# Reordering the first steps, regrouping the last batch and moving the last residuals in a top-k attention and MLP kernel

## The chip, the cores and the metric

The program runs on one core of a Trainium2 chip. The metric is the device time of one execution in microseconds; lower is better. The engines are named as the profile names them: PE is TensorE (PEld is its loading of weights), DVE is VectorE, ACT is ScalarE, POOL is GpSimd and SP is SyncE, which issues most of the DMAs.

## The reference, cut to what matters

There are 8 batches, 8 heads, 576 rows and a head size of 64, all in float32. For each row the 32 largest of 576 scores are kept, and the rest take no part in the softmax. The heads are laid side by side (512 columns), and a normalised MLP of width 2048 with a residual follows. `moe_g_ln` and the two weight matrices arrive as float64.

```python
scores = scale * np.matmul(q, k.transpose(0, 1, 3, 2))
kth = np.partition(scores, -top_k, axis=-1)[..., -top_k:-top_k + 1]
scores = np.where(scores >= kth, scores, -1000000000.0)
attn = np.exp(scores - np.max(scores, axis=-1, keepdims=True))
attn = attn / (np.sum(attn, axis=-1, keepdims=True) + 1e-09)
x = np.matmul(attn, v)                       # then heads side by side: (8, 576, 512)
xn = (x - mu) / np.sqrt(var + 1e-06) * g_ln
out = x + np.maximum(xn @ w_ch1, 0.0) @ w_ch2
```

## The kernel before, in words

**Tiles, jobs and units.** The 576 rows of a batch are four tiles of 128 rows, numbered 0 to 3, and a rest of 64 rows, numbered `J` (4). Two heads are handled together, so a batch has four head pairs (`hp`). A *unit* is one row tile of one head pair; a *group* is the list of tiles whose attention is multiplied with the values at once; a *job* is one group of one head pair. `parts` says how a batch is cut: batch 0 in `[0,1]`, `[2,3]`, `[J]`; batch 1 in `[0,1]`, `[2,3,J]`; batches 2 to 7 in `[0,1,J]`, `[2,3]`. For each part all four head pairs come in turn, which gives N = 160 units.

**The steps.** The program is one long loop over steps `n`, written out by hand; each engine executes its own instructions in the order in which they are issued. In step `n`, unit `n` goes through `select` on DVE, in four calls; unit `n+1` is prepared for it; earlier units are masked, exponentiated, turned and multiplied with the values. The parts that matter here are:

- `scores(u)`: eight products on PE into four PSUM tiles (L354), which ACT copies to `sc` (L335). `due(n)` says whose scores step `n` makes: those of unit n+1 in the early steps, of unit n+2 after step 17.
- `halve(u)`: of the two halves of every row of scores, DVE takes the elementwise maximum `hi` (L375); POOL works out the minimum `lo` from integers, as a subtraction and an addition (L376, L379).
- `select(u, 0)` takes 16 candidates out of `lo`; `select(u, 1)` to `select(u, 3)` take the 32 largest out of `hi` and those candidates (MAX8 and MATCH_REPLACE8, L391, L386, L399).
- `move(u)` turns a unit's weights by two DVE transposes (L468) and DMAs through DRAM, `turn(u)` by PE transposes (L490) and ACT copies (L502). A unit is `moved` from batch 2 on, if it is neither a rest nor the last of its group.
- `values(g)` multiplies a group with its values (L544, L551); `place(g)` turns the result back and puts it into `x` (L583, L560).

**The weights.** Each of 32 pieces of the float64 weights is converted by the kernel: `fetch` (a DMA), `split` (three or four ACT operations L183 to L189, then a clamp on POOL, L190), `shift` (a left shift by three bits on DVE, L193) and `join` (two POOL operations, L199 and L201). `batches` puts four pieces ahead of the loop and then one or two into each of the steps 0 to 15; `weights(n, 0)` and `weights(n, 1)` issue them. The shifts and joins of a batch are issued one step after its splits, in `weights(n, 1)`, after `halve(nxt)`.

**The MLP and its planner.** When all four head pairs of a part are done, their rows become a `Block` of one to three row tiles. `give(n)` puts its products into the list `todo`: transposes of `x` ("turn"), 64 products for the hidden layer ("hidden", L664) whose moving side has 128 columns for each tile of the block, and 16 products of 512 columns for each tile ("project", L680). After the last product of a tile, ACT scales (L689), POOL adds the residual (L693), and SP stores. Eight calls of `fill()` in every step take products out of `todo`: each call adds `share[0]` to a credit `owed[0]`, which is held at 6.0 at most, and products are issued while the credit covers half their planned cost. `slot(n)` sets the share. Up to step 17 it is the difference of planned DVE and PE costs; after that it spreads what is in `todo` evenly over the steps up to each coming give, keeps a reserve of 4 us, and takes the least of these:

```python
                if m > n:
                    even = min(even, (left - RESERVE) / (m - n))
                    left += sum(b.cost() for b in gives[m])
```

The first block is given at step 9 (`gives_first`), the others at 19, 31, 44, 55 and so on; the last two of batch 7 are a block of three tiles (tiles 0 and 1 with the last rows of batches 6 and 7) at step 156 and a block of two at step 163. The loop ends with step 165.

**The lead-in.** Before the loop the kernel loads, turns and scores the first head pair, calls `halve(units[0])`, `load_gain()` and the splits of the four first pieces (`weights(-1, 0)`, `weights(-1, 1)`).

Of the kernel before, what the change touches and what calls it, by code (L numbers as in the profile page):

```python
# [10 lines left out]
ALU = mybir.AluOpType  # L11
# [10 lines left out]
J = 4  # L22
# [7 lines left out]
def kernel(  # L30
# [41 lines left out]
    nc = tc.nc  # L72
    P = nc.NUM_PARTITIONS
    B, H, S, D = q.shape
# [130 lines left out]
    now = [-1]  # L205
# [5 lines left out]
    def load_gain():  # L211
        ps = turned()
        nc.tensor.transpose(ps[:, 0:NC], grow[:], ident[0:NC, 0:NC])
        nc.scalar.copy(gcol[:], ps[:, 0:NC])


    batches = {}
# [5 lines left out]

    def weights(n, phase):

        now, before = batches.get(n, []), batches.get(n - 1, [])
        if phase == 0:
            for x in batches.get(n + 1, []):
                x.fetch()
            for x in now[0::2]:  # L230
                x.split()
        elif phase == 1:
            for x in before:
                x.shift()
            for x in before:
                x.join()
            for x in now[1::2]:
                x.split()
# [5 lines left out]
    share = [0.0]  # L244
    owed = [0.0]
# [83 lines left out]
    def scores(u):  # L329

        u.sc = scpool.tile([P, 2, S], FP32, tag="sc", name="sc")
        made = [score_half(u, s) for s in range(2)]
        for t in range(len(u.tiles)):
            for s in range(2):
                nc.scalar.copy(  # L335
                    u.sc[:, t, s * HALF : (s + 1) * HALF], made[s][t][:, 0:HALF]
                )
# [25 lines left out]
    def halve(u):  # L363

        nt = len(u.tiles)  # L370
        u.lo = lopool.tile([P, 2, HALF], FP32, tag="lo", name="lo")
        u.hi = hipool.tile([P, 2, HALF + TOP_K // 2], FP32, tag="hi", name="hi")
        a, b = u.sc[:, 0:nt, 0:HALF], u.sc[:, 0:nt, HALF:S]
        lo, hi = u.lo[:, 0:nt], u.hi[:, 0:nt, 0:HALF]
        nc.vector.tensor_tensor(hi, a, b, ALU.max)  # L375
        nc.gpsimd.tensor_tensor(  # L376
            lo.bitcast(I32), a.bitcast(I32), hi.bitcast(I32), ALU.subtract
        )
        nc.gpsimd.tensor_tensor(lo.bitcast(I32), lo.bitcast(I32), b.bitcast(I32), ALU.add)  # L379
# [215 lines left out]
    class Block:  # L595
# [40 lines left out]
        def items(self):  # L636
            n = self.n
            N = n * P
# [38 lines left out]
            def project(i, f):  # L677
                if f == 0:
                    ps[i] = product("ops")
                nc.tensor.matmul(  # L680
                    ps[i][:],
                    hT[f][:, i * P : (i + 1) * P],
                    w2[:, f, :],
                    start=(f == 0),
                    stop=(f == NF - 1),
                )
                if f == NF - 1:
                    o = opool.tile([P, DM], FP32, tag="o", name="o")
                    nc.scalar.activation(  # L689
                        o[:], ps[i][:], AF.Identity,  # L690
                        bias=self.mv[:, i, 0:1], scale=self.rstd[:, i : i + 1],
                    )
                    nc.gpsimd.tensor_tensor(o[:], o[:], self.x[i], ALU.add)  # L693
                    for dst, rows in self.dsts[i]:
                        stores.append(lambda d=dst, s=o[rows, :]: nc.sync.dma_start(d, s))

# [33 lines left out]
    for b in range(B):  # L730
        parts = [[0, 1], [2, 3], [J]]
        if b:
            parts = [[0, 1], [2, 3]]
            parts[b < 2].append(J)
        for qts in parts:
            jobs += [Job(b, hp, [qts]) for hp in range(NHP)]
    units = []
# [7 lines left out]
    N = len(units)  # L745
# [11 lines left out]
    CONVERTING = max(n for n in batches if batches[n]) + 2  # L757
# [16 lines left out]
    for j in jobs:  # L774
        if j.hp == NHP - 1:
            b = j.b
# [23 lines left out]
    def at(i):  # L800
        return units[i] if 0 <= i < N else None
# [6 lines left out]

    def due(n):

        ahead = [n + 1] if n < CONVERTING else [n + 2]
        if n == CONVERTING:
            ahead = [n + 1, n + 2]
        return [units[i] for i in ahead if i < N]
# [5 lines left out]
    for j in fresh[1:]:  # L820
        before = jobs[jobs.index(j) - 1]
# [32 lines left out]
    def slot(n):  # L854


        if n <= CONVERTING:
            return max(0.0, dve_cost(n) - pe_cost(n)) / SLOTS
        left = sum(t[1] for t in todo)
        if n > last_give:  # L860
            even = left / max(1, END - 1 - n)
        else:
            even = 99.0
            for m in sorted(gives):
# [3 lines that stand above are left out]
        return max(0.0, even) / SLOTS  # L868
# [8 lines left out]
    gives_first = min(gives)  # L877
# [7 lines left out]
    load(fresh[1], nc.sync, nc.scalar)  # L885
    scores(units[0])
    halve(units[0])
    load_gain()
    weights(-1, 0)
    weights(-1, 1)  # L890
    for n in range(END):
        now[0] = n
        if n in gives:
            give(n)
        share[0] = slot(n)
        u, nxt, mk = at(n), at(n + 1), at(n - 1)
        ex, g = after(n)
        g = g if g and not g.quick else None
# [38 lines left out]
            keep_den(ex)  # L937
        if u:
            select(u, 1)
        if nxt:  # L940
            halve(nxt)
        for den in recips.pop(n, []):
# [101 lines left out]
```

## Time and profile before

| What | Before |
| --- | --- |
| Device time, median of 4 runs | 1660.4 us (1657.11 to 1660.88) |
| Device time of the profiled execution | 1660.76 us |
| Span of the profiled execution | 1658.3 us |
| Granted PE clock, mean | 0.978 |
| PE busy | 1560.5 us, 94% of the span |
| DVE busy | 1474.5 us, 89% |
| ACT busy | 1038.0 us, 63% |
| POOL busy | 675.0 us, 41% |

The span is measured from the first to the last instruction in the profile; the device time is 2.5 us more in the same execution. Times below are in microseconds from the start of the span unless a duration is meant. A row of the timeline gives the start, the length, the engine, the line, the operation with its output and inputs, the number of instructions, and in brackets how long the engine stood idle before it and who ended that. PE matmul rows overlap: each instruction's end is modelled, so the spacing from one start to the next tells the rate.

### The profile page before, as it was taken

To read this page: it belongs to the slowest core of one execution; us is meant where nothing else is said; L and a number is where in the kernel's file an instruction comes from. 1 tells how busy PE (TensorE), PEld (TensorE's weight loads), DVE (VectorE), ACT (ScalarE), POOL (GpSimd) and SP (SyncE) were. 2 spreads that over 40 slices of the span, in tenths; PEclk is the share of its full clock that TensorE was granted. 3 is DMA by queue.
4 is the path that set the end of the run, shared out by engine and by line. 5 is a ranking of instruction groups with operands and counts; after the bars stand their busy time and mean duration, and the time that the engine had idled before them with its cause. 6 is when DMAs were issued, how large, how long until landed. Compare 5 with 4: busy or idle time off the path is not lost.

```text
span 1658.3 us, 24475 instructions
## 1 busy us (share of the span) xinstructions
PE 1560.5 (94%) x6825; PEld 919.2 (55%) x6825; DVE 1474.5 (89%) x4619; ACT 1038.0 (63%) x2607; POOL 675.0 (41%) x879
## 2 busy tenths in 40 slices
PE   2668989989899999999999999999999999999998
PEld 1336457456455475755547575655547565755564
DVE  5997999999999999999999999999999999997000
ACT  6886877767656666666656665666656665665310
POOL 5776763343333434334343433344343433343010
PEclk9879999999999999999999999999999999999999
DMA  7423333001433334333443325333443334232100
GB/s 177 105 71 95 88 60 62 22 14 23 95 104 97 92 87 120 100 101 79 120 114 102 86 80 138 91 92 84 115 118 98 86 83 122 90 92 72 32 13 13
DMA packets 301199, 142.28 MB, mean 86 GB/s; under 512 B 246276, under 2 KB 283144, under 8 KB 301064
## 3 DMA queue, kind: packets, MB, share of 16 engines
q1 hardware_dynamic: 296328, 140.13, 31.9%
q10 hardware_dynamic: 4736, 0.59, 0.3%
q8 instruction: 55, 0.90, 0.2%
q14 instruction: 80, 0.66, 0.1%
HBM read 93.46 MB, written 47.19 MB: 85 GB/s over the span
## 4 chain that ended last, share of the span: by engine, by line
PE 66%; DVE 20%; ACT 5%; issue 4%; POOL 2%; DMA 1%; SPq 0%; ACTq 0%; POOLq 0%; DVEq 0%
PE hps L664 24%; PE ops L680 23%; PE scps L354 8%; PE av L544 6%; DVE m L399 6%; DVE hi L386 5%; DVE hi L391 3%; PE av L551 2%; PE tp L490 2%; DVE lo L386 2%; DVE hi L375 2%; ACT e L426 1%; ACT sc L335 1%; DVE size L193 1%; PE tp L648 1%
## 5 line engine op out<-in xcount | busy, mean ns | idle before, releaser
L664 PE MATMUL hps<-xT,w 128*128 128x256 f32 (+1 forms) x2048 | 551.4, 413 | 6.2 <-ACT xT L653 6.2
L680 PE MATMUL ops<-w,h 128*128 128x512 f32 x1152 | 548.8, 603 | 0.0
L399 DVE MAX8 m<-hi 128x8 f32<-128x304 f32 x1152 | 489.1, 461 | 3.3
L664 PEld LDWEIGHTS hps<-xT,w 128*128 128x128 f32 x2048 | 373.2, 192 | 122.7 <-issue 31.9
L376 POOL TENSOR_TENSOR lo<-sc,hi 128x576 int32<-128x576 int32 (+1 forms) x160 | 208.2, 1301 | 481.9 <-DVE hi L375 238.2
L386 DVE MATCH_REPLACE8 hi<-m,hi 128x304 f32<-128x304 f32 x864 | 390.6, 458 | 0.0
L680 PEld LDWEIGHTS ops<-w,h 128*128 128x128 f32 x1152 | 200.7, 192 | 186.4 <-issue 181.4
L354 PE MATMUL scps<-kT,qT 64*128 64x288 f32 (+3 forms) x1344 | 219.8, 429 | 35.3 <-DVE qT L306 26.5
L391 DVE MAX8 hi<-lo 128x8 f32<-128x288 f32 x576 | 234.0, 443 | 12.8 <-POOL lo L379 11.7
L335 ACT COPY sc<-scps 128x288 f32<-128x288 f32 x576 | 199.7, 408 | 70.9 <-PE scps L354 56.5
L426 ACT ACTIVATE e<-sc,m 128x576 f32<-128x576 f32 x288 | 224.1, 779 | 6.1 <-DVE m L399 4.0
L436 ACT ACTIVATE e<-e,bias 128x576 f32<-128x576 f32 x288 | 224.8, 781 | 0.6
L379 POOL TENSOR_TENSOR lo<-lo,sc 128x576 int32<-128x576 int32 (+1 forms) x160 | 207.3, 1296 | 12.6
L354 PEld LDWEIGHTS scps<-kT,qT 64*128 64x128 f32 (+1 forms) x1344 | 122.0, 179 | 152.3 <-issue 60.3
L675 ACT ACTIVATE h<-hps 128x512 f32<-128x512 f32 (+1 forms) x160 | 89.2, 557 | 95.3 <-PE hps L664 94.1
L544 PE MATMUL av<-pt,vb 128*64 128x256 f32 (+2 forms) x1088 | 147.8, 414 | 0.2 <-ACT pt L513 0.2
L375 DVE TENSOR_TENSOR hi<-sc 128x576 f32<-128x576 f32 (+1 forms) x160 | 116.7, 729 | 21.9 <-ACT sc L335 21.9
L386 DVE MATCH_REPLACE8 lo<-hi,lo 128x288 f32<-128x288 f32 x288 | 125.6, 443 | 0.0
L693 POOL TENSOR_TENSOR o<-o,x 128x512 f32<-128x512 f32 x32 | 42.2, 1320 | 199.9 <-ACT o L689 199.9
L556 ACT COPY oT<-av 128x256 f32<-128x256 f32 (+2 forms) x68 | 26.2, 386 | 148.9 <-PE av L551 148.9
L544 PEld LDWEIGHTS av<-pt,vb 128*64 128x64 f32 x1088 | 73.8, 142 | 77.9 <-ACT sc L335 15.9
L490 PE MATMUL tp<-ident,e 128*128 128x128 f32 x576 | 92.1, 285 | 25.0 <-ACT e L436 24.5
(70 smaller groups left out, 1257.9 us busy)
## 6 DMA issues: line engine op xcount, KB each, us to landing
turned<-sc SPq DMA_DIRECT2D x72, 512.0 KB, 2.6
pt<-turned SPq DMA_DIRECT2D x288, 128.0 KB, 3.0
vb<-in_v_dram SPq DMA_DIRECT2D x136, 128.0 KB, 2.7
raw<-in_moe_w_ch_dram SPq DMA_DIRECT2D x32, 512.0 KB, 4.0
kin<-in_k_dram SPq DMA_DIRECT2D x128, 72.0 KB, 2.6
qin<-in_q_dram SPq DMA_DIRECT2D x120, 72.0 KB, 2.7
out_dram<-o SPq DMA_DIRECT2D x32, 256.0 KB, 2.2
ends<-in_v_dram SPq DMA_DIRECT2D x136, 16.0 KB, 2.4
```

Of the source, the lines that this page charges most:

```text
L335: nc.scalar.copy(u.sc[:, t, s * HALF : (s + 1) * HALF], made[s][t][:, 0:HALF])
L354: nc.tensor.matmul(ps[i * R : i * R + ql, o : o + width], qT[r, q0 : q0 + ql], kT[r, k0 : k0 + width], start=True, stop=True,)
L376: nc.gpsimd.tensor_tensor(lo.bitcast(I32), a.bitcast(I32), hi.bitcast(I32), ALU.subtract)
L379: nc.gpsimd.tensor_tensor(lo.bitcast(I32), lo.bitcast(I32), b.bitcast(I32), ALU.add)
L386: nc.vector.match_replace(x[:, t], m[:, t, :], x[:, t], LOWEST)
L391: nc.vector.max(u.hi[:, t, o : o + 8], u.lo[:, t])
L399: nc.vector.max(m[:, t, :], u.hi[:, t])
L426: nc.scalar.activation(u.e[:, t], u.sc[:, t], AF.Prelu, bias=u.thr[:, t, 7:8], scale=-1.0, alpha=SLOPE)
L436: nc.scalar.activation(u.e[:, t], u.e[:, t], AF.Exp, bias=u.bias[:, t : t + 1], scale=-scale / SLOPE, accum_out=g.den[:, col : col + 1],)
L544: nc.tensor.matmul(av[h * D : (h + 1) * D, 0 : g.nq], vb[:, h * J + c, :], g.blocks[:, h, 0 : g.nq // 32, c, :], start=(c == 0), stop=False,)
L664: nc.tensor.matmul(ps["h"][:, o : o + N], w1[:, c, f * P : (f + 1) * P], xT[0][:, c, 0:N], start=(c == 0), stop=(c == NC - 1),)
L680: nc.tensor.matmul(ps[i][:], hT[f][:, i * P : (i + 1) * P], w2[:, f, :], start=(f == 0), stop=(f == NF - 1),)
```

## The change

It has five parts.

1. The scores of unit 1 are issued ahead of the loop, right after `halve(units[0])` and before `load_gain()` and the splits of the first four pieces; `due(0)` is empty.
2. For unit 0 alone, `lo` is made by DVE as a minimum instead of by two POOL operations.
3. The shifts of a batch of pieces leave `weights(n, 1)` and are issued in step `n` after `select(u, 1)` and before `halve(nxt)`.
4. In step `gives_first` (9) the credit `owed[0]` is set to zero and the share is halved.
5. The last batch is cut in `[0,J]`, `[1,2]`, `[3]` instead of `[0,1,J]`, `[2,3]`: twelve jobs instead of eight, still twenty units. Its blocks have two tiles (tile 0 and the last rows), two tiles (1 and 2) and one tile (3), given at steps 152, 159 and 163. Residuals issued after step N (160) are added by DVE instead of POOL.

```diff
@@ weights
         elif phase == 1:
-            for x in before:
-                x.shift()
             for x in before:
                 x.join()
@@ halve
         nc.vector.tensor_tensor(hi, a, b, ALU.max)
+        if u.i == 0:
+            nc.vector.tensor_tensor(lo, a, b, ALU.min)
+            return
         nc.gpsimd.tensor_tensor(
             lo.bitcast(I32), a.bitcast(I32), hi.bitcast(I32), ALU.subtract
         )
@@ project
-                    nc.gpsimd.tensor_tensor(o[:], o[:], self.x[i], ALU.add)
+                    engine = nc.vector if now[0] > N else nc.gpsimd
+                    engine.tensor_tensor(o[:], o[:], self.x[i], ALU.add)
@@ jobs
         if b:
             parts = [[0, 1], [2, 3]]
-            parts[b < 2].append(J)
+            if b == B - 1:
+                parts = [[0, J], [1, 2], [3]]
+            else:
+                parts[b < 2].append(J)
@@ due
-        ahead = [n + 1] if n < CONVERTING else [n + 2]
+        ahead = [] if n == 0 else [n + 1] if n < CONVERTING else [n + 2]
@@ lead-in
     scores(units[0])
     halve(units[0])
+    scores(units[1])
     load_gain()
@@ loop
         share[0] = slot(n)
+        if n == gives_first:
+            owed[0] = 0.0
+            share[0] /= 2
...
         if u:
             select(u, 1)
+        for x in batches.get(n - 1, []):
+            x.shift()
         if nxt:
             halve(nxt)
```

## The prediction

> **What bounds the kernel now.** I read the page's 40 slices first, to see where an engine is short of work.
>
> ```profile
> PE   2668989989899999999999999999999999999998
> ...
> DVE  5997999999999999999999999999999999997000
> ...
> PEclk9879999999999999999999999999999999999999
> ```
>
> Three stretches differ. In the first tenth PE has gaps while DVE is full; then both are full; in the last 120 us PE works alone. The sums by stage put numbers to it (columns: window, length, then PE, PEld, DVE, ACT and POOL busy with instruction counts, granted clock, DMA share, GB/s).
>
> ```profile
> 10.00:20.00 10.00, 2.76 (x11) 1.37 (x9) 4.78 (x15) 8.17 (x17) 4.64 (x5) 1.00 0.88 203
> 20.00:30.00 10.00, 2.29 (x8) 1.26 (x8) 5.91 (x7) 7.32 (x15) 5.75 (x6) 1.00 0.49 113
> ...
> 130.00:140.00 10.00, 10.00 (x44) 8.67 (x43) 5.86 (x23) 4.23 (x8) 4.51 (x5) 0.93 0.17 52
> 480.00:1500.00 1020.00, 1015.03 (x4470) 591.09 (x4467) 1005.35 (x3159) 649.64 (x1676) 397.23 (x557) 1.00 0.36 99
> 1530.00:1653.00 123.00, 123.00 (x413) 70.79 (x411) 3.93 (x10) 27.05 (x59) 8.10 (x12) 1.00 0.06 19
> ```
>
> From 480 us PE lacks 5 us in 1020, and from 1530 on it lacks none. The end is therefore PE's: the time is PE's work plus PE's gaps, and the gaps lie in the first 480 us. A change can gain by shortening the start, where DVE or a chain through several engines sets the pace, and pays for every product that it adds later, even where DVE is relieved. DVE's timeline shows its waits at the start.
>
> ```profile
> 15.83 0.82 DVE L391 MAX8 hi<-lo 128x8 f32<-128x288 f32 x2 [3.02 <-POOL lo L379]
> ...
> 24.09 0.76 DVE L375 TENSOR_TENSOR hi<-sc 128x576 f32<-128x576 f32 x1 [4.24 <-ACT sc L335]
> ...
> 26.12 5.22 DVE L193 TENSOR_SCALAR size<-size 128x512 uint32<-128x512 uint32 x4
> ...
> 40.15 0.76 DVE L193 TENSOR_SCALAR size<-size 128x512 uint32<-128x512 uint32 x2
> ...
> 143.06 0.76 DVE L375 TENSOR_TENSOR hi<-sc 128x576 f32<-128x576 f32 x1 [7.20 <-ACT sc L335]
> 143.73 2.39 DVE L193 TENSOR_SCALAR size<-size 128x512 uint32<-128x512 uint32 x2
> ```
>
> A pair of shifts takes 0.76 us at 40.15 and 2.39 us at 143.73. The slow ones lie beside POOL's subtraction and addition for `lo`, the fast pair beside a clamp. PE's timeline gives the burst behind the 7.20 us, and the rates for the last batch.
>
> ```profile
> 127.33 13.48 PE L664 MATMUL hps<-xT,w 128*128 128x256 f32 x52 [2.98 <-ACT xT L653]
> ...
> 1522.94 1.95 PE L544 MATMUL av<-pt,vb 128*64 128x256 f32 x16
> ...
> 1596.15 1.04 PE L648 MATMUL tp<-ident,x 128*128 128x128 f32 x8
> 1597.03 1.02 PE L680 MATMUL ops<-w,h 128*128 128x512 f32 x2
> 1597.92 27.89 PE L664 MATMUL hps<-xT,w 128*128 128x256 f32 x128
> 1625.65 27.63 PE L680 MATMUL ops<-w,h 128*128 128x512 f32 x64
> ```
>
> **The start, step by step.** I follow DVE's queue; a step begins with its first MAX8 on `lo`. Step 0 began at 15.83. With the minimum on DVE (spacing of the like L375: 0.67 us) the 3.02 us wait becomes 0.67, and step 0 begins at 13.4. `select(u,0)` takes 2.3 us and `select(u,1)` 1.65: 17.4. Then come the four shifts. Each needs its piece's clamp; the splits on ACT begin some 0.6 us later than now (13.7 against 13.1), because unit 1's four copies stand ahead of them, and take 2.43 us a piece, so the fourth clamp ends at 22.1 and the fourth shift at 22.5. The scores of unit 1 are long there, so `hi` follows at once (23.2), the two transposes (1.35) and the rest of the step (4.3): step 1 begins at 28.8 instead of 35.5. Not all of this lasts. In step 1 the shift of batch 0 now stands ahead of `halve`, and its second piece is clamped on POOL behind the four joins (eight operations, 10.3 us, from 27.6). DVE waits at that shift until 38.5; queued behind it are `hi` of unit 2 and two selects. Step 2 begins at 43.85 instead of 45.11, and the gain is 1.3 us.
>
> In steps 2 to 9 DVE never waits (0.14 us in all), so each shorter shift counts. Before `halve`, POOL has no `lo` to work on, and I take the fast spacing, 0.33 us a piece. The slow pairs took 1.85 in steps 3 and 5 and 2.31 in step 9, the slow single of step 2 0.78: gains of 1.2, 1.2, 1.6 and 0.5. With the 1.3 that makes 5.8 us at step 10.
>
> Step 9 issues the first block's products. The credit stood at its cap of 6.0, so the planner's arithmetic gives 26 hidden products, the 52 instructions of the burst (two per product). Step 10's scores stand behind them on PE: hence 7.20 us. With no credit and half the share (3.6 instead of 7.2) only 6 products are issued. The other 20 come later; at 0.216 us an instruction they are 8.6 us. The wait goes; the next thing late is the shift itself (0.67, now ahead of `hi`). At `hi` of step 10 I have 5.8 + 7.2 - 0.7 = 12.3 us.
>
> In steps 10 to 13 `hi` follows `hi` every 12.56 us, and DVE idles 1.26. The loop is not DVE's: POOL's subtraction, addition and first join (5.7 us), then ACT, whose `sign` waits for that join and holds back a copy that frees PSUM for the scores. Shorter shifts gain nothing there; I put these steps at nothing, 1 us either way.
>
> The 20 products must not come back on the path. By the planner's arithmetic 3.5 of their 8.8 planned us are made up in step 18 and the rest by step 31; PE stood idle 4.30 us in step 19 and 5.05 in step 31, waiting for rows, which come earlier now. I cost them at nothing; without that cover they cost 8.6. Step 44 has another such gap (5.29), so what DVE has gained by then shifts everything after it. **Start: -12**, bounds -4 and -17 (the upper if the loop shortens by a shift's excess of 1.6 us in three steps).
>
> **The last batch.** Columns first: hidden layers of three and two tiles take 0.323 and 0.217 us an instruction (20 from 1532.14 to the next operation at 1538.59; 128 from 1597.92 to 1625.65); two, two and one take 0.217, 0.217 and x, 128 times each. No row has 128 moving columns with fresh weights in this operation. The nearest are the transposes at 1596.15, which load 128x128 weights for each 128 columns: (1.04 - 0.27)/7 = 0.11. So +0.3 us with the unrounded spacings (0.3225, 0.2166, 0.1087). The other bound is a weight load's own recorded length, 0.19: +10.7. I take the transposes, whose shape is the same.
>
> The Trainium skill (TensorE: Matmul & The Clock Gate, section "Back-to-back issue gap") says that at 128 columns the spacing in a stream of weight loads and matmuls is set by both, about 81 ns where the matmul alone would give about 56. By that ratio, an estimate from the page, the spacing here would be 0.16 and the block 6.4 us dearer; the sum would be 1658.
>
> Regrouping leaves tile 2 the last of its group: 4 units go from `move` to `turn`. PE gains eight transposes of 0.11 each, 0.87 a unit: **+3.5**. ACT gains two copies of 0.58 a unit, but is busy 27 of the last 123 us. DVE loses 4 x 1.4 us and SP twenty DMAs, off the path there. Four more groups: 256 columns take 2.42 us from the start at 1522.94 to the next operation, 320 take 2.95 elsewhere, so 0.30 is fixed: **+1.2**. One more block boundary: +0.3. Four more loads of values on SP lie two steps ahead of their use. Together **+5.3**.
>
> The last residual, on DVE at some 0.65 instead of POOL's 1.26, is on the path after the last product: **-0.6**. DVE waits there for ACT's result; behind it stand the statistics of the last tile, but the two-tile block leaves 15 projects (13 us) after its first residual, against some 4 us for that chain.
>
> The new gives also raise the planned fill from 6.4 to 7.1 us a step from step 116 on, and 35 instead of 58 us are left at the last give. PE hardly waits there now, so this only moves work; it can fill the 1.1 and 0.6 us that PE idles in steps 117 and 157: **-1.5**.
>
> Sum, against the profiled execution's 1660.8: -12 + 5.3 - 0.6 - 1.5 gives **1652**. Its median is 1660.4, 0.4 lower; I leave that aside.
>
> **The rivals.**
> *The postponed products return on the path.* PE has 11.4 us of work a step in steps 11 to 13 already (12.56 less about 1.2 idle), and its gaps at 19 and 31 may be rows' latency. Against it: two more gaps. Then the start gives 12 - 8.6, about 4: 1660, no change.
> *The loop shortens too.* If the sooner subtraction on POOL, free of the shift, pulls ACT's `sign` forward, up to 17: 1647. Against it: the contention took only some 0.2 us from POOL in each step.
> *Weights bind the one-tile block.* Place: 128 instructions after the last attention product. Price: up to 10.4 us more. With a start gain of 6 instead of 12 it ends at 1668. It decides above 0.18 us an instruction if the start gives 9. For it: the recorded 0.19 and the missing row; against it: the transposes.
> That DVE's relief in the last batch shortens the time itself I rule out: DVE is done at 1530 and PE at 1653.
>
> **How the numbers follow.** The forecast, 1648 to 1657, has 0.55; the shorter loop, below 1648, 0.15; the returning products 0.18; the weights 0.12. A measurement here can tell about 0.2%, 3.3 us, from no change: faster 0.70, same 0.18, slower 0.12. The range 1645 to 1663 leaves out most of the slower case and the far end of the shorter loop.
>
> **What would show it.** Right: step 1's first MAX8 on `lo` near 28.8 us; a wait of DVE near 33 us for a clamp; shifts of 0.8 us a pair; no 7 us wait near step 10; 128 hidden instructions of 128 columns in about 14 us; last product some 8 us earlier. Wrong: PE gaps in steps 19 and 31 unchanged with the same end; spacing of 0.16 or more; new gaps on PE after step 150.

## The result, and the profile after

The changed kernel takes 1656.7 us (median of 39 runs, 1654.9 to 1658.8), against 1660.1 us for the kernel before on the same chip (59 runs). The ratio is 0.9981, with an interval of 0.9976 to 0.9985: 3.2 us faster. The forecast was 8.4 us faster, so the direction was right and the size was not. The profiled execution has a span of 1655.8 us against 1658.3, 2.5 us less.

The page's slices first, as before: PE, DVE and the granted clock in 40 equal parts of the span.

```profile
PE   3569999999899999999999999999999999999998
...
DVE  5998899999999999999999999999898997888400
...
PEclk6678999999999999999999999999999999999999
```

From the fourth slice to the tenth PE shows 9 throughout, where it had three 8s. DVE, which had been done at slice 37, now has gaps from slice 29 on and works until slice 38. The clock of the first slices reads lower than before (6678 for 9879), but that is no difference between the two executions: in the trace of the kernel before, the records of the clock begin only at 59.76 us, and time without a record is counted as full clock. PE's timeline shows the same pace in both, 2.29 us for the eight products of one unit's scores (the row before, then the row after); at full clock they take 1.24 us (the row at 129.10 below):

```profile
26.34 2.29 PE L354 MATMUL scps<-kT,qT 64*128 64x288 f32 x8 [11.18 <-DVE qT L306]
24.69 2.29 PE L354 MATMUL scps<-kT,qT 64*128 64x288 f32 x8 [11.72 <-DVE qT L306]
```

The same windows as before (window, length, then PE, PEld, DVE, ACT and POOL busy with counts, granted clock, DMA share, GB/s):

```profile
10.00:20.00 10.00, 2.97 (x11) 1.82 (x9) 6.10 (x18) 9.05 (x20) 1.84 (x3) 0.79 0.85 196
20.00:30.00 10.00, 2.29 (x8) 1.26 (x8) 8.35 (x28) 6.83 (x13) 6.59 (x7) 0.50 0.67 143
130.00:140.00 10.00, 9.30 (x50) 7.38 (x47) 9.41 (x34) 7.83 (x18) 8.60 (x9) 1.00 0.49 134
480.00:1500.00 1020.00, 1013.71 (x4474) 598.18 (x4472) 972.62 (x3054) 634.22 (x1627) 384.40 (x544) 1.00 0.35 95
1530.00:1650.00 120.00, 118.59 (x557) 77.08 (x556) 20.20 (x70) 37.22 (x86) 13.21 (x22) 1.00 0.06 17
```

At the start DVE's busy time in 20 to 30 us rises from 5.91 to 8.35, and in 130 to 140 from 5.86 to 9.41: the two stretches in which it had waited. In the body PE's busy time is 1.3 us *less* in 1020 than before, and from 1530 on PE is idle for 1.4 us where it had not been idle at all. That is the first sign of where the gain went, and one that the forecast had named as a sign of being wrong: new gaps on PE after step 150.

DVE's timeline at the start:

```profile
12.39 0.75 DVE L378 TENSOR_TENSOR lo<-sc 128x576 f32<-128x576 f32 x1
13.18 0.82 DVE L395 MAX8 hi<-lo 128x8 f32<-128x288 f32 x2
...
22.10 0.43 DVE L193 TENSOR_SCALAR size<-size 128x512 uint32<-128x512 uint32 x1 [1.65 <-POOL size L190]
...
28.72 0.81 DVE L395 MAX8 hi<-lo 128x8 f32<-128x288 f32 x2
...
38.35 0.82 DVE L193 TENSOR_SCALAR size<-size 128x512 uint32<-128x512 uint32 x1 [4.33 <-POOL size L190]
...
121.59 0.76 DVE L193 TENSOR_SCALAR size<-size 128x512 uint32<-128x512 uint32 x2
...
133.01 0.76 DVE L375 TENSOR_TENSOR hi<-sc 128x576 f32<-128x576 f32 x1
```

Read against the forecast: step 0 at 13.18 (forecast 13.4), the fourth shift at 22.10 (22.1), step 1 at 28.72 (28.8), the wait for the clamp until 38.35 (38.5). The pair of shifts that took 2.38 us at 125.25 before takes 0.76 at 121.59, and `hi` at 133.01 follows without the 7.20 us wait.

PE's timeline, with the places that the rest of this text needs:

```profile
124.29 4.87 PE L668 MATMUL hps<-xT,w 128*128 128x256 f32 x12 [2.98 <-ACT xT L657]
129.10 1.24 PE L354 MATMUL scps<-kT,qT 64*128 64x288 f32 x8
...
745.74 5.19 PE L668 MATMUL hps<-xT,w 128*128 128x384 f32 x10 [3.45 <-ACT xT L657]
...
1391.91 0.63 PE L652 MATMUL tp<-ident,x 128*128 128x128 f32 x4 [0.83 <-ACT sc L335]
...
1482.42 2.86 PE L668 MATMUL hps<-xT,w 128*128 128x256 f32 x12 [1.08 <-ACT xT L657]
...
1560.58 1.78 PE L668 MATMUL hps<-xT,w 128*128 128x256 f32 x7 [1.41 <-ACT xT L657]
...
1622.86 14.54 PE L668 MATMUL hps<-xT,w 128*128 128x128 f32 x128
1637.24 13.90 PE L684 MATMUL ops<-w,h 128*128 128x512 f32 x32
```

The first block starts with 12 hidden instructions (6 products) instead of 52, and the scores follow at 129.10. The one-tile block takes 14.38 us for 128 instructions, 0.112 each. New are waits for `xT`, the copy of a turned `x`, in front of hidden layers at 1482 and 1560 and a longer one at 745.74.

The gain over the kernel before can be followed along the steps by the start of each step's first MAX8 on `lo`: 4.2 us at step 10, 12.4 at step 11, 12.6 at step 20, 10.3 at step 21, 13.1 at step 33, 12.2 at step 60, 10.1 at step 84. The drop at step 21 is a new wait of DVE for `lo`, and POOL's timeline shows why: the residual of the first block waits there for ACT and stands ahead of the subtraction for `lo`.

```profile
234.97 1.27 POOL L699 TENSOR_TENSOR o<-o,x 128x512 f32<-128x512 f32 x1 [6.72 <-ACT o L693]
236.20 1.40 POOL L380 TENSOR_TENSOR lo<-sc,hi 128x576 int32<-128x576 int32 x1
239.12 0.82 DVE L395 MAX8 hi<-lo 128x8 f32<-128x288 f32 x2 [3.07 <-POOL lo L383]
```

The rise at step 33 is a wait of the same kind (2.74 us, at 357.32 in step 32) that the kernel before had and the changed one has not. One execution's gain at the start is less certain than its digits: the kernel with the start only (below) has the same PE instructions as the changed one up to 800 us and is 13.1 instead of 12.4 us ahead at step 11 and 13.6 instead of 12.2 at step 60; the kernel with the regrouping only has those of the kernel before up to 810 us and is 3.2 us ahead of it at step 11.

The scores of unit 116, the last ones before the new gives change the pace, begin 10.1 us earlier on PE. From there on DVE's steps say nothing (they fall behind because the planner issues more products a step), and PE's own account is needed. The table adds up the distances from one PE instruction to the next, by kind, from the scores of unit 116 to the last product; waits are in the kind that stands in front of them.

| Kind of instruction | Before | After | Difference |
| --- | --- | --- | --- |
| scores | 51.87 | 52.79 | +0.92 |
| transposes of weights (L490) | 13.97 | 17.55 | +3.58 |
| values (L544, L551) | 56.74 | 56.61 | -0.13 |
| turning of x (L648) | 6.53 | 8.15 | +1.62 |
| hidden | 198.98 | 199.11 | +0.13 |
| project | 215.50 | 217.36 | +1.86 |
| others | 11.81 | 11.80 | -0.01 |
| sum | 555.41 | 563.37 | +7.96 |

So the profiled executions say: 10.1 us gained by unit 116's scores, 8.0 lost after them, 0.3 gained behind the last product.

### The profile page after: what moved, and what is told of

Read it like the earlier page. It is cut to its first block, busy times and chain, and to the rows that moved or that the text cites. A ratio compares the mean times of both kernels' runs of the same rounds, so it can differ in the third digit from the quotient of the medians.

```text
span 1655.8 us, 24949 instructions
## 1 busy us (share of the span) xinstructions
PE 1563.8 (94%) x7057; PEld 941.7 (57%) x7057; DVE 1459.3 (88%) x4617; ACT 1044.6 (63%) x2619; POOL 667.6 (40%) x878
## 4 chain that ended last, share of the span: by engine, by line
PE 61%; DVE 30%; ACT 3%; POOL 3%; issue 1%; DMA 1%; DVEq 0%; ACTq 0%; POOLq 0%
PE hps L668 23%; PE ops L684 21%; DVE m L403 9%; DVE hi L390 8%; PE scps L354 7%; PE av L548 5%; DVE hi L395 5%; DVE lo L390 3%; DVE hi L375 2%; PE tp L494 2%; PE av L555 2%; DVE sc L472 1%; POOL lo L383 1%; POOL lo L380 1%; ACT sc L335 1%
## 5 line engine op out<-in xcount | busy, mean ns | idle before, releaser
L668 PE MATMUL hps<-xT,w 128*128 128x256 f32 (+2 forms) x2176 | 556.4, 400 | 9.1 <-ACT xT L657 9.1
L668 PEld LDWEIGHTS hps<-xT,w 128*128 128x128 f32 x2176 | 388.0, 192 | 116.5 <-issue 34.2
L548 PE MATMUL av<-pt,vb 128*64 128x256 f32 (+4 forms) x1152 | 149.1, 401 | 0.0
L560 ACT COPY oT<-av 128x256 f32<-128x256 f32 (+4 forms) x72 | 26.8, 372 | 161.6 <-PE av L555 161.6
L375 DVE TENSOR_TENSOR hi<-sc 128x576 f32<-128x576 f32 (+1 forms) x160 | 115.1, 719 | 12.2 <-ACT sc L335 12.1
L548 PEld LDWEIGHTS av<-pt,vb 128*64 128x64 f32 x1152 | 77.7, 143 | 79.8 <-ACT sc L335 16.4
L472 DVE STREAM_TRANSPOSE sc<-e 128x512 f32<-128x512 f32 x136 | 90.1, 689 | 33.5 <-ACT e L440 33.3
L494 PE MATMUL tp<-ident,e 128*128 128x128 f32 x608 | 96.6, 283 | 23.3 <-ACT e L440 23.3
```

Of the source, the lines that this page charges most:

```text
L548: nc.tensor.matmul(av[h * D : (h + 1) * D, 0 : g.nq], vb[:, h * J + c, :], g.blocks[:, h, 0 : g.nq // 32, c, :], start=(c == 0), stop=False,)
L668: nc.tensor.matmul(ps["h"][:, o : o + N], w1[:, c, f * P : (f + 1) * P], xT[0][:, c, 0:N], start=(c == 0), stop=(c == NC - 1),)
```

## The experiments

Theory A: the start gives what was forecast and loses some 2 us in the body; the last batch costs 8 us instead of the forecast net of 3. Theory B: PE has slack in the body, so the start's gain does not reach the end, and the last batch costs little. Differences below are worked out from the ratio to the kernel before (1659 to 1660 us in each comparison), with its interval.

### The two halves and the residual

**Start only**, parts 1 to 4 of the change:

```diff
@@ weights
-            for x in before:
-                x.shift()
@@ halve
+        if u.i == 0:
+            nc.vector.tensor_tensor(lo, a, b, ALU.min)
+            return
@@ due
-        ahead = [n + 1] if n < CONVERTING else [n + 2]
+        ahead = [] if n == 0 else [n + 1] if n < CONVERTING else [n + 2]
@@ lead-in
+    scores(units[1])
@@ loop
+        if n == gives_first:
+            owed[0] = 0.0
+            share[0] /= 2
...
+        for x in batches.get(n - 1, []):
+            x.shift()
```

> Parts 1 to 4 alone; the last batch is cut as before and the residuals stay on POOL. Theory A (the start gives its forecast 12 us, two of them are lost by a slow clock spell near 745 us, and the last batch costs about 8): 10 to 12 us faster than before, ratio 0.9928 to 0.994, and no lost time behind step 120. Theory B (the start's gain does not reach the end, because PE is the bound behind it): 3 to 5 us faster, ratio 0.997 to 0.998, with PE idle for less and DVE waiting for more between steps 20 and 110.

Measured: 1651.2 us, ratio 0.9947 (0.9935 to 0.9960), 8.8 us faster; the span is 10.2 us shorter. A little short of theory A, and far from theory B. The start does reach the end.

**Regrouping only**:

```diff
-            parts[b < 2].append(J)
+            if b == B - 1:
+                parts = [[0, J], [1, 2], [3]]
+            else:
+                parts[b < 2].append(J)
```

> Only the last batch is cut in [0,J], [1,2], [3]; all else as before. Theory A: 7 to 9 us slower, ratio 1.0042 to 1.0054, made of some 3.6 us of transposes that replace moves and 4 us of waits of PE for the copied x at the two new block boundaries. Theory B: at most 2 us slower, ratio up to 1.001.

Measured: 1667.0 us, ratio 1.0044 (1.0032 to 1.0057), 7.3 us slower. PE needs 563.08 us from unit 116's scores on, nearly as in the full change. Theory A. The waits are there without the start's edits too (PE's timeline of this kernel):

```profile
1488.51 5.45 PE L664 MATMUL hps<-xT,w 128*128 128x256 f32 x24 [1.07 <-ACT xT L653]
...
1566.66 5.88 PE L664 MATMUL hps<-xT,w 128*128 128x256 f32 x26 [1.40 <-ACT xT L653]
```

**Residual only**:

```diff
-                    nc.gpsimd.tensor_tensor(o[:], o[:], self.x[i], ALU.add)
+                    engine = nc.vector if now[0] > N else nc.gpsimd
+                    engine.tensor_tensor(o[:], o[:], self.x[i], ALU.add)
```

> Only the residuals behind step 160 go to DVE. Both theories: 0.3 to 0.6 us faster, the difference of two adds of 128x512 on the path after the last product; within what can be measured it is no change, ratio 0.9996 to 1.0.

Measured: 1659.9 us, ratio 0.9999 (0.9990 to 1.0008). This run tests nothing, and that is a finding about the code. POOL's timeline still has both last residuals:

```profile
1640.27 1.26 POOL L694 TENSOR_TENSOR o<-o,x 128x512 f32<-128x512 f32 x1 [39.16 <-ACT o L689]
1653.95 1.26 POOL L694 TENSOR_TENSOR o<-o,x 128x512 f32<-128x512 f32 x1 [12.42 <-ACT o L689]
```

In that method `N` is not the number of units: a line at its head sets `N = n * P`, the columns of the block. So the description of the change above ("after step N (160)") is wrong: the condition holds where the step is past 128 times the block's tiles, which happens only in the new one-tile block. Without regrouping the edit moves nothing, and the run is a repeat of the kernel before; its interval of 0.09% to either side shows the noise. In the changed kernel one residual moves (DVE's timeline):

```profile
1652.03 0.69 DVE L699 TENSOR_TENSOR o<-o,x 128x512 f32<-128x512 f32 x1 [41.07 <-ACT o L693]
```

From the end of the last product to the end of the span, the regrouped kernel without it needs 5.3 us and the changed kernel 4.7: the forecast 0.6, where it acts.

**The four units that are turned instead of moved**, alone:

```diff
         u.moved = not u.rest and u is not u.group.units[-1]
+        if u.job.b == B - 1 and u.qt == 1:
+            u.moved = False
```

> Before, but tile 1 of batch 7 is turned on PE instead of moved by DVE, so four units change as in the new last batch, with the old groups and blocks. Theory A: 3.5 us slower (32 transposes of 0.11 us), ratio 1.002. If transposes are free there because PE only waits in other places (theory B): no change.

Measured: 1663.6 us, ratio 1.0023 (1.0014 to 1.0031), 3.8 us slower. In PE's account the transposes rise by 3.50 us and nothing else changes. So half of what the regrouping costs is this term, as forecast. Of the other 4 us in the regrouped kernel's account, most are PE's waits: those over 0.3 us add up to 4.9 us there and to 2.0 in the kernel before. About 1 us more is work, in the values of the four more groups.

### The start taken apart

**Credit only** (part 4):

```diff
         share[0] = slot(n)
+        if n == gives_first:
+            owed[0] = 0.0
+            share[0] /= 2
```

> Only the planner's edit at step 9 (credit to zero, share halved), all else as before. Theory A, the start is a sum of terms: the forecast's own term, the 7.20 us wait of DVE at the scores of step 10 goes and the shift's wait of about 0.7 stays, so 6 to 7 us faster than before. Theory B, the parts overlap and the 20 postponed products come back: within 2 us of before, with PE's waits in steps 19 and 31 shorter by what the start gained. If most of the whole start edit's 8.7 us is here, the other edits hardly matter.

Measured: 1656.5 us, ratio 0.9979 (0.9971 to 0.9988), 3.5 us faster: between the theories. DVE's steps show how it goes: 9.6 us ahead at step 11, 7.5 at step 16, 5.7 at step 21, 7.3 at step 60, 5.2 at step 84. DVE's timeline has new, shorter waits where the old one was and where the list of products now ends later:

```profile
147.60 0.76 DVE L375 TENSOR_TENSOR hi<-sc 128x576 f32<-128x576 f32 x1 [2.84 <-ACT sc L335]
...
243.68 0.82 DVE L391 MAX8 hi<-lo 128x8 f32<-128x288 f32 x2 [2.56 <-POOL lo L379]
```

**Shifts only** (part 3):

```diff
@@ weights
-            for x in before:
-                x.shift()
@@ loop
             select(u, 1)
+        for x in batches.get(n - 1, []):
+            x.shift()
         if nxt:
```

> Only the shifts moved (from the weights' phase 1 to between the second select and the next halve). Theory A: pairs of shifts fall from 1.9 and 2.4 us to 0.75 us, 4 to 4.5 us by step 10 as in the forecast; in step 1 no wait of 4 us, since step 1 begins at 35.5 there and the clamp ends at 38. Then 4 us faster. Theory B: the 20-product burst's end sets step 10's scores whatever DVE does before it, and the 7.20 us wait takes up what the shifts gave: under 1 us faster.

Measured: 1653.5 us, ratio 0.9963 (0.9951 to 0.9976), 6.1 us faster, more than theory A's 4. DVE's timeline:

```profile
122.05 0.74 DVE L193 TENSOR_SCALAR size<-size 128x512 uint32<-128x512 uint32 x2
...
139.18 0.76 DVE L373 TENSOR_TENSOR hi<-sc 128x576 f32<-128x576 f32 x1 [6.23 <-ACT sc L333]
```

The big wait moves earlier with DVE instead of absorbing its gain (6.23 us, until 139.18 instead of 143.06), and the pair of 2.39 us that stood right behind it is gone as well: 4.2 us at step 10 become 6.2 at step 11 and 7.0 at step 15.

**Lead only** (parts 1 and 2):

```diff
@@ halve
+        if u.i == 0:
+            nc.vector.tensor_tensor(lo, a, b, ALU.min)
+            return
@@ due
-        ahead = [n + 1] if n < CONVERTING else [n + 2]
+        ahead = [] if n == 0 else [n + 1] if n < CONVERTING else [n + 2]
@@ lead-in
+    scores(units[1])
```

> Only unit 1's scores ahead of the loop and unit 0's lo as a minimum on VectorE. Theory A: step 0 begins at 13.4 and step 1 at 28.8, but unit 2's work follows the clamp of the second piece on POOL at 38.5, so 1.3 to 2 us are left at step 2 and at the end. Theory B: POOL and ACT, which have the fetched weights to convert, lead through steps 1 to 9 and nothing is left: within 1 us of before.

Measured: 1658.7 us, ratio 0.9992 (0.9983 to 1.0001). The profile has step 1 8.2 us earlier, step 2 1.3, and 1.2 from there to the end. Neither the time nor one profile can tell that from nothing, but both agree with 1.3.

**Lead and shifts without the credit** (parts 1, 2 and 3; the two diffs above together):

> The start without its planner edit: unit 1's scores ahead, unit 0's minimum on VectorE, shifts moved; credit and share as before, last batch as before. Alone the shifts gave 6.1 us and the lead 1.3, the planner's edit 3.4, all three together 8.7. Theory A, shifts and lead add up and the planner's edit gives only what is left of the 7.20 us wait after the postponed products came back: 7 to 7.5 us faster than before, with the 7 us wait of VectorE still at step 10 and PE's wait near 742 at 2 us instead of 3.4, at full clock. Theory B, the parts cover one another: 6 us or less.

Measured: 1652.9 us, ratio 0.9960 (0.9948 to 0.9973), 6.6 us faster; between the theories. PE's wait near 742 is short here:

```profile
750.98 3.49 PE L665 MATMUL hps<-xT,w 128*128 128x384 f32 x10 [1.98 <-ACT xT L654]
```

Together with the start only, the planner's edit is worth 2 us on top of the others (by the spans, 3.7), not 7.2.

### The block boundaries

When a block is given, six projects of the one before are meant to stay between the turning of the new `x` and its hidden layers, while ACT copies it. The code cuts the list at `len(todo) - 6`. With four or five products left this index is negative, and Python counts it from the list's end, so with five left one project stays behind the turning, and with four left two do. By the planner's arithmetic four or five are left at steps 44, 76, 116 and at all gives of the last batch. PE's timeline of the changed kernel agrees: two or four project instructions (one or two projects) lie there between turning and hidden layers, and twelve at the other gives after the first.

**Regrouping with the cut corrected at every give**:

```diff
-            kept, last = todo[: len(todo) - at_end], todo[len(todo) - at_end :]
+            cut = max(0, len(todo) - at_end)
+            kept, last = todo[:cut], todo[cut:]
```

> The last batch regrouped as in the change, and the slice at a give that keeps back up to six projects corrected, so that with four or five left all of them lie between the turning of x and the new hidden layers, instead of one or two (this also holds at the gives of steps 44, 76 and 116). Theory A, PE's waits for the copied x at block boundaries are some 4 of the 7 us that the regrouping costs: 3 to 4 us slower than before, with waits under 0.3 us at the boundaries of steps 152 to 163. Theory B, the waits only move to the turning itself or to the next boundary: 6.5 to 7.5 us slower, as with the regrouping alone.

Measured: 1667.4 us, ratio 1.0047 (1.0034 to 1.0059), 7.8 us slower: by the total, theory B. But the trace says otherwise of the place in question. PE needs 559.45 us from unit 116's scores on, 3.6 less than with the regrouping alone, and the loss is at step 44:

```profile
457.72 1.12 PE L648 MATMUL tp<-ident,r 128*128 128x128 f32 x4 [7.52 <-POOL r L619]
458.63 6.44 PE L680 MATMUL ops<-w,h 128*128 128x512 f32 x10
```

There the turning itself waits for rows, until 457.63 before and 457.72 now. Before, projects ran ahead of that wait (5.29 us); now they stand behind it, and everything after them is 4 us later. A run whose total shows no gain can hold two effects of opposite sign.

**The changed kernel with the cut corrected from step 110 on**:

```diff
-            at_end = 0 if early else 6
+            at_end = 0 if early else 6 if n < 110 else min(6, len(todo))
```

> The changed kernel, with the slice at a give corrected from step 110 on only (so that all of the up to six kept projects lie between the turned x and its hidden layers at steps 116, 152, 159 and 163; the early gives, where the correction cost 4 us at step 44, stay). Theory A, the block boundaries' waits for the copied x are 3.6 us of the last batch's 8: 3.5 us faster than the changed kernel, that is about 1653, 6.5 to 7 under before. Theory B, the waits come back elsewhere: within 1 us of the changed kernel.

Measured: 1654.7 us, ratio 0.9972 (0.9961 to 0.9982) to the kernel before, so 1.5 us better than the change by the ratios, whose intervals overlap: between the theories. PE's account, 563.05, is only 0.3 less than in the changed kernel. At step 116 a longer wait came up, and half clock behind it (10 instructions in 5.18 us; 3.49 at full clock):

```profile
1120.60 5.18 PE L668 MATMUL hps<-xT,w 128*128 128x384 f32 x10 [2.33 <-ACT xT L657]
```

**The same from step 150 on** (150 for 110 in the diff):

> The changed kernel with the slice corrected from step 150 on only, that is at the last batch's boundaries 152, 159 and 163; step 116 stays as in the changed kernel. Theory A, of the 8 us that the last batch costs, 3.6 are PE's waits for the copied x at these boundaries, and the correction from step 110 on gave less only because of a new wait of 2.3 us and half clock at 1120: 3.5 us faster than the changed kernel, 1653; PE from unit 116's scores to its last product near 559.6 us instead of 563.4. Theory B, the postponed projects cost elsewhere what the boundaries gain: within 1 us of the changed kernel.

Measured: 1654.2 us, ratio 0.9968 (0.9956 to 0.9979), 5.3 us faster than before and 2.1 better than the change, with intervals that just overlap; PE's account falls by 2.4, to 560.98. Theory A in kind, two thirds of it in size. The project row of the account falls from 217.36 to 214.25; turning of `x` (8.29) and scores (52.89) stay dear. PE's timeline at step 152, with ten project instructions where there were two, and no wait:

```profile
1476.13 4.46 PE L684 MATMUL ops<-w,h 128*128 128x512 f32 x10
1480.43 2.32 PE L668 MATMUL hps<-xT,w 128*128 128x256 f32 x10
```

**The kernel before with the cut corrected from step 110 on** (the same diff):

> The kernel before with nothing but the slice corrected from step 110 on. Theory A, the boundaries' waits are there before the change too, whatever the start does: 1 to 3 us faster than before (the start alone gained 3.2 from it). Theory B, it was the start's planner edit that opened these waits, and it alone gains from the correction: within 1 us of before.

Measured: 1658.0 us, ratio 0.9992 (0.9983 to 1.0001). PE's account falls by 2.5 us, to 552.87, but the time alone doesn't tell it from nothing. Waits at boundaries were there before the change; regrouping adds a boundary to them.

### What the start loses near 742, and a better version

**Start only, cut corrected from step 110 on**:

> Start only (all parts but the last batch and the residual), with the same correction from step 110 on. Theory A: the start alone lost 1.3 us at the last batch's boundaries and 1 more near 1118: 1.5 to 2 us faster than the start alone, about 1649. Theory B: nothing, 1651.

Measured: 1647.1 us, ratio 0.9924 (0.9911 to 0.9936), 12.6 us faster than the kernel before, 3.8 better than the start alone. The planner's edit had made the boundaries dearer (PE's account 556.7 with it, in both kernels that have it without regrouping, 555.4 without); now the account is 552.88.

**The same, cut corrected from step 76 on** (70 for 110 in the diff):

> As the last, with the correction from step 76 on, so that four instead of two projects lie ahead of PE's wait near 742. Theory A, that wait (3.4 us with the start's edit, 2 before) and the half clock of 3.4 us after it cost 2 us of the start's gain, and two projects of 1.7 us together bring the wait under the length after which the clock fell: 2 us faster than with the correction from 110 on, about 1647, no half clock near 742. Theory B, PE only reaches its next wait sooner, since VectorE sets the pace there: the same time within 0.7 us, though the clock stays.

Measured: 1646.4 us, ratio 0.9923 (0.9910 to 0.9935): the same. But theory B's clock did not stay either; the wait at 742 became two, 1.06 and 2.63 us, and half clock came again:

```profile
744.64 4.54 PE L665 MATMUL hps<-xT,w 128*128 128x384 f32 x8 [2.63 <-ACT xT L654]
```

So this run could not tell the theories apart.

**The same with twice the planner's reserve**:

```diff
-    RESERVE = 4.0
+    RESERVE = 8.0
```

> Start with the correction from step 76 on and twice the planner's reserve (8 instead of 4 us of projects left at each give). Theory A, more projects ahead of a boundary take up PE's wait near 742 (1.06 and 2.63 us, then half clock): waits under 1.2 us, full clock, and 1 to 2 us faster than with the reserve of 4, about 1645. Theory B, VectorE sets the pace there and PE's wait is slack: the same 1646 to 1647, or slower by what the longer reserve adds at the early boundaries.

Measured: 1641.9 us, ratio 0.9896 (0.9881 to 0.9911), 17.3 us faster than the kernel before. It is the best version here, faster than both kernels. PE's timeline at the place:

```profile
734.37 0.66 PE L649 MATMUL tp<-ident,r 128*128 128x128 f32 x4
734.86 3.60 PE L681 MATMUL ops<-w,h 128*128 128x512 f32 x8
738.64 0.66 PE L491 MATMUL tp<-ident,e 128*128 128x128 f32 x4 [0.18 <-ACT sc L333]
739.13 1.88 PE L681 MATMUL ops<-w,h 128*128 128x512 f32 x4
740.85 0.81 PE L665 MATMUL hps<-xT,w 128*128 128x384 f32 x2
```

Twelve project instructions (six projects) lie between the turning and the hidden layers, and the wait for `xT` and the half clock are gone. DVE's gain goes from 11.1 (reserve of 4) to 18.4 us at step 84 and from 11.6 to 14.8 at step 21: the early boundaries gained as well. The wait near 742 was not slack: from the scores of unit 78 to those of unit 80, PE's gain over the kernel before falls from 14.4 to 11.2 us with the reserve of 4 and rises from 19.1 to 21.7 with that of 8. The reserve grows at every give, so this run doesn't price that one place, and no run has the longer reserve without the other edits.

## Why the prediction was right or wrong, point by point

**The first two steps: right.** Every instant of the chain through the clamps fell within 0.3 us, and of 6.8 us at step 1 only 1.1 was left at step 2, against 1.3 forecast.

**The shifts: right in mechanism, too large in sum.** 4.2 us at step 10 instead of 5.8. Steps 2, 3 and 5 gave 0.7, 1.2 and 1.4 us (forecast 0.5, 1.2 and 1.2), and a pair takes 0.69 us from its start to the next operation, about as forecast. But step 9 gave 0.9 instead of 1.6, and step 8 lost 0.8: its shift takes 1.46 us at its new place (107.84), against 0.39 before. The kernel with the start only, whose instructions are the same there, loses nothing in step 8 and is 5.0 us ahead at step 10.

**The 7.20 us wait: right, but the number by luck.** The wait is gone, six products instead of 26 are issued. At `hi` of step 10, for which the forecast gave 12.3, the gain is 10.05 us (143.06 to 133.01). The 12.4 appear only at step 11, because the pair of 2.39 us that stood behind `hi` is shorter and ahead of it now, a gain that the forecast had put at nothing.

**"I cost them at nothing": failed.** The postponed products did come back on the path, though not as PE's work in steps 19 and 31, where the forecast looked for them. The first block ends later against the steps, so its residual on POOL falls ahead of a `lo` that DVE needs: 12.6 us at step 20 are 10.3 at step 21. The kernels without the planner's edit lose at most 0.2 there, the one with that edit alone 1.8, and with the reserve of 8 nothing is lost. That the wait of step 32 is gone gives 2.8 back; a wait for `lo` of 1.35 us at 454.12, again behind a residual, takes 1.2. Then comes PE's wait for `xT` near 742, 3.45 us instead of 1.95, and half clock after it. A window of the changed kernel shows it (granted clock third from the end):

```profile
746.00:748.00 2.00, 2.00 (x4) 0.96 (x4) 2.00 (x6) 1.32 (x4) 1.55 (x2) 0.56 0.77 183
```

DVE's steps lose 1.7 us there, in the start alone and in the credit alone too, and not in the kernels without that edit. ACT's timeline shows the longer wait: ahead of the copy of `xT` (at 745.06, before at 756.82) stand copies of scores that wait for DVE, first in the changed kernel, then in the kernel before:

```profile
743.89 1.31 ACT L335 COPY sc<-scps 128x288 f32<-128x288 f32 x4 [3.11 <-DVE m L403]
755.65 1.31 ACT L335 COPY sc<-scps 128x288 f32<-128x288 f32 x4 [1.62 <-DVE m L399]
```

PE is 13.25 us ahead of the kernel before at that point and DVE 11.76, so PE waits 1.5 us longer. The forecast's own rival, that these products return on the path, was right in kind with a third of its price: 12.6 us at step 20 are 10.1 at step 84. With the credit alone, 1.3 us more go at the last boundaries (account 556.7 against 555.4).

**The hidden columns: right.** 0.112 us an instruction at 128 columns; the transposes were the right row, and the rival with the weights fell. The Trainium skill's ratio of 81 to 56 (TensorE: Matmul & The Clock Gate, "Back-to-back issue gap"), which gave an estimate of 0.16, is not seen for these shapes.

**Four units turned: right.** +3.58 in the account, 3.5 forecast, and 3.8 measured by itself.

**Four more groups: the work nearly right, the sum not.** A group of 128 columns takes 1.35 us from 1553.84 to the next operation, and 0.30 plus half of 2.12 would be 1.36. The account shows -0.13 instead of +1.2, because the values' row in the kernel before also holds two waits of 0.46 us for the copy of their result that the changed kernel does not have. Without them the row rises by 0.8.

**"One more block boundary: +0.3" and the body's pacing, -1.5: failed, and this is the larger part.** These two made -1.2 together. In the account their rows (project, turning of `x`, scores) are +4.4. The forecast took a boundary for a switch between products, and counted PE's waits of 1.1 and 0.6 us in steps 117 and 157 as room to fill. The wait at step 117 did shrink, to 0.2 us, but waits of 1.08 and 1.41 us came up at the new boundaries, 1482 and 1560. What a boundary costs is a chain: PE turns `x`, ACT copies it, PE waits for what the projects left over do not cover. The cut that was meant to keep six products keeps one or two when the list is short, and the forecast overlooked that case. Correcting it at the last batch removes both waits and gives back 2.4 us of the profile's account (2.1 in the time). What makes turning `x` and the scores 2.5 us dearer was not taken apart by an experiment, so that part of the cause stays open: the waits of 0.41 and 0.83 us for ACT at 1309 and 1391 are half of it, and the scores' 0.9 is there with the credit alone too (52.82).

**The last residual: right in size, by luck in its place.** 0.6, though the condition means something other than I had read.

The sum, by the profile: -12 became -10.1, +5.3 - 1.5 became +8.0, and -0.6 became -0.3 from the last product on; together -2.5 instead of -8.8. That the start came within 2 us of its forecast is partly luck: the shifts gave less, the pair behind `hi` gave more, and the postponed products took 2.5. Start only (-8.8) and regrouping only (+7.3) add up to -1.5 in the times, with intervals of about 2 us each, which holds the change's -3.2.

## What to carry to other kernels

A boundary between two stages of a software pipeline has a price of its own, the latency of the hand-over (here PE, ACT, PE), and it is hidden only by work that is left over at that moment: count what the code really leaves, at every boundary, before counting operations. An edit that only postpones work moves what follows that work, in every engine's queue: here its cost lay in a residual on POOL and a wait at step 76, not where the work was. And where a total shows nothing, look at the place itself in the trace: a correction that gained 3.6 us where it was meant to act lost 4 us at another boundary.

## What the runs showed of the hardware that was not expected

Half clock follows some of PE's waits of 2 to 3 us, and not by their length alone. After a wait of 2.62 us (regrouping with the cut corrected) eight instructions of 384 columns took 2.85 us; after 2.63 us (the row at 744.64) they took 4.54; after 2.33 us (the row at 1120.60) the clock fell as well, and after 1.95 us in the kernel before it did not.

```profile
761.39 2.85 PE L664 MATMUL hps<-xT,w 128*128 128x384 f32 x8 [2.62 <-ACT xT L653]
```

The Trainium skill (TensorE: Matmul & The Clock Gate, "What's actually happening") says that activity is judged in windows of 3413 ns that run freely and don't start anew with the kernel. The clock records of the traces agree: in every run, each spell of half clock that begins after 100 us lasts 3.41, 6.83 or 10.24 us, but for the last one, which the program's end cuts off, and all of a run begin on one grid of 3.41 us. On that grid the wait of 2.63 us (742.01 to 744.64) lies inside one window, and the next one runs at half clock:

```profile
741.99:745.40 3.41, 0.78 (x4) 0.49 (x4) 3.41 (x10) 2.61 (x7) 0.05 (x1) 1.00 0.43 133
745.40:748.81 3.41, 3.41 (x7) 1.89 (x6) 3.41 (x13) 0.82 (x3) 3.33 (x3) 0.50 0.81 142
```

The wait of 2.62 us (758.77 to 761.39) is cut by an edge, which leaves 0.81 us of it in one window and 1.82 in the next, and the clock stays:

```profile
756.17:759.58 3.41, 2.60 (x7) 0.81 (x5) 3.41 (x12) 0.04 (x1) 0.00 (x0) 1.00 0.38 154
759.58:763.00 3.42, 1.61 (x5) 1.06 (x6) 3.42 (x10) 3.39 (x9) 0.91 (x1) 1.00 0.54 153
763.00:766.41 3.41, 3.41 (x14) 2.10 (x13) 3.41 (x14) 1.70 (x4) 3.16 (x3) 1.00 0.81 131
```

No limit in microseconds follows from this: at the start of the changed kernel half clock also came after a wait of 1.57 us (140.51 to 142.09). One window at half clock cost 1.7 us, half its length: ten instructions took 5.18 us at 1120.60 instead of 3.49, and DVE's steps lost as much by the one near 742.

A shift of 128 x 512 words takes 0.42 us alone and 0.76 in a pair in the changed kernel, and 2.38 for a pair beside POOL's work on `lo` in the kernel before. Moving the shifts ahead of `halve` was worth 6.1 us, the largest single part of this change.
